# The normalizer of linear attention on VectorE and ScalarE in place of TensorE matmuls and a DRAM broadcast

## The chip, the cores and the metric

The kernel runs on one core of a Trainium2 chip. The metric is the device time of one execution in microseconds (us). "PE" is TensorE, "PEld" its weight loads, "DVE" VectorE, "ACT" ScalarE, "POOL" GpSimd and "SP" SyncE, which only starts DMAs here. Each engine works through its own queue in order; a semaphore holds an instruction until what it reads has been written.

## The reference

```python
x = A_x                                        # 2048 tokens, 512 features
g = sigmoid((x * gate_w).sum(-1, keepdims=True))
# branch a: linear attention, 32 heads of 16
q, k, v = heads(x @ wqkv)
phi = lambda t: where(t > 0, t + 1, exp(t)) + 1e-6
kv  = einsum("bhsd,bhse->bhde", phi(k), v)
z   = einsum("bhsd->bhd", phi(k))
num = einsum("bhqd,bhde->bhqe", phi(q), kv)
den = einsum("bhqd,bhd->bhq", phi(q), z)[..., None] + 1e-6
a   = merge(num / den) @ wo
# branch b: layer norm of x, then an MLP over the tokens (1792 hidden), gelu
b   = transpose(gelu(einsum("bsd,sf->bdf", layernorm(x), w1) + b1) @ w2 + b2)
out = g * a + (1 - g) * b
```

The change concerns `den`: for each token and head, one sum over the head's 16 features of phi(q) times z. The kernel divides phi(q) by it before the last product, which gives the same as dividing num.

## The kernel before, in words

Everything is kept in SBUF. `NT` = 16 tiles of 128 tokens, `ND` = 4 blocks of 128 features (8 heads each), `NF` = 14 blocks of 128 hidden units, `SC` = 512 tokens, `NSC` = 4 chunks of that size. The order on each engine is the order in which the code is written out (`manual_schedule`); nothing reorders it.

1. *K stage* (up to 33.7 us). For each token tile: x @ wk on PE (`k_part`), phi on ACT and DVE (`phi`, L216 to L220) into `pk`, statistics for the layer norm, and, four tiles behind, G = x^T phi(k) (`g_tile`), kept in four PSUM banks and copied to `gT`.
2. *Q loop* (33.7 to 57.9 us). For t = 0..15: three matmuls for the first three hidden blocks (`NB0` = 3, j = 0..2) and one block of q with its phi, into `pqT`, which holds phi(q) with features on partitions and tokens along the free axis: `pqT[:, j, tokens]`. From t = 6 on, `z_add` (L281) adds one tile of phi(k) per step into `zacc`. Behind the loop come the last five `z_add`s (L425) and `z_column` (L426, its body L354 to L369): a transpose in blocks of 32x32, sums and small copies, which give `zcol` (z by feature, on partitions) and `Z32` (z spread so that one column belongs to one head).
3. *Hidden loop* (57.9 to 97.85 us). For j = 3..13: 16 matmuls into a bank `uacc`, then the gelu on ACT (L329) into `uT`. Behind j = 6 stand `kv_matmuls` (64 small matmuls, then the product `kvT` on DVE, L348), `den_matmuls` (16 matmuls of 32 output rows in four column tiles, then a reciprocal on DVE, L404), `w2_matmuls` (16 matmuls of 32x32 tiles, whose weights are `kvT`), the 16 gate sums on DVE (L431), and `rden_chunk` for chunks 0 and 1. `w2_copies` (ACT, L391) follow behind j = 6..9 and give `W2sb`.
4. *Output loop* (97.85 us to the end). For each token tile t: four matmuls of `pqT` with `W2sb` into a bank `aps`, scaled on ACT into `a_sc` (L492); 14 matmuls of `uT` with w2 into a bank `yps`; DVE joins both into `ot` (L505), and a DMA writes it out. `rden_chunk` for chunks 2 and 3 stands behind tiles 1 and 2.

`rden_chunk(c)` brings the reciprocal onto phi(q): the reciprocals, one row per head, go to DRAM once (L440), and for each feature block a DMA on POOL's queue reads 8 rows back with each one repeated over 16 partitions (`rex`, L444); DVE multiplies `pqT` by it (L446).

All PSUM tiles come from one pool of eight banks (`bank`); a matmul that opens a new tile waits until the reader of that bank's earlier tile is through. All matmuls are issued by the helper `mm` and so carry L113; the tile's name tells them apart.

Of the kernel before, what the change touches and what calls it, by code (L numbers as in the profile page):

```python
# [7 lines left out]
ACT = mybir.ActivationFunctionType  # L8
ALU = mybir.AluOpType
AX = mybir.AxisListType  # L10
BF16 = mybir.dt.bfloat16
FP32 = mybir.dt.float32
# [3 lines left out]
def kernel(  # L16
# [13 lines left out]
    nc = tc.nc  # L30
    P = nc.NUM_PARTITIONS
    EPS = 1e-5
    PHI_EPS = 1e-6
    HEAD = 16
# [3 lines left out]
    S, D = X.shape  # L38
    F = B_w1.shape[1]
    NT = S // P  # L40
    ND = D // P
    NF = F // P
    SC = 512
    NSC = S // SC
# [16 lines left out]
    wpool = ctx.enter_context(tc.tile_pool(name="wstream", bufs=4))  # L61
    work = ctx.enter_context(tc.tile_pool(name="work", bufs=3))
    opool = ctx.enter_context(tc.tile_pool(name="opool", bufs=4))
    dpool = ctx.enter_context(tc.tile_pool(name="dpool", bufs=1, space=bass.MemoryType.DRAM))
    ps = ctx.enter_context(tc.tile_pool(name="ps", bufs=8, space=bass.MemoryType.PSUM))

    def keep(shape, dtype, name):
        return persist.tile(shape, dtype, name=name, tag=name)

    def bank(name, dtype=FP32):  # L70
        return ps.tile([P, SC], dtype, name=name, tag="bank")

    xs = keep([P, NT, D], BF16, "xs")
# [6 lines left out]
    pqT = keep([P, ND, S], BF16, "pqT")  # L80
# [1 line left out]
    uT = keep([P, NF, D], BF16, "uT")  # L82
    kvT = keep([P, ND, Q32], BF16, "kvT")
    W2sb = keep([P, ND, D], BF16, "W2sb")
    Z32 = keep([P, ND * 40], BF16, "Z32")
    zacc = keep([P, D], FP32, "zacc")
    zT = keep([P, D], FP32, "zT")
    zpart = keep([P, NZ], FP32, "zpart")
    zquad = keep([Q32, NQ, NZ], FP32, "zquad")
    zsum = keep([Q32, NZ], FP32, "zsum")  # L90
    zcol = keep([P, ND], FP32, "zcol")
    rden = keep([P, SC], BF16, "rden")
    ident = keep([P, P], BF16, "ident")
    maskH = keep([P, 8], BF16, "maskH")
    maskQ = keep([P, 2], BF16, "maskQ")
    gw_b = keep([P, D], BF16, "gw_b")
# [6 lines left out]
    gpre = keep([P, NT], FP32, "gpre")  # L103
# [8 lines left out]
    def mm(o, lhsT, rhs, start, stop, **kw):  # L112
        nc.tensor.matmul(o, lhsT=lhsT, rhs=rhs, start=start, stop=stop, **kw)  # L113
# [29 lines left out]
    for k, q in ((1, nc.scalar), (2, nc.sync), (3, nc.scalar)):  # L143
        load_wk(q, k)
    nc.vector.memset(ones_f[:], 1.0)
    nc.vector.memset(mhalf[:], -0.5)
    nc.vector.memset(Z32[:], 0.0)
    nc.gpsimd.memset(ident[:], 0.0)
    nc.gpsimd.affine_select(
        out=ident[:], in_=ident[:], compare_op=ALU.not_equal, fill=1.0, base=0,  # L150
# [5 lines left out]
        out=maskQ[:], in_=maskH[:].rearrange("p (a m) -> p m a", m=2), op=ALU.max, axis=AX.X  # L156
# [4 lines left out]
        out=xT[:, :, 3 * P : 3 * P + 2],  # L161
        in_=xs[:, 0, 0 : 2 * ND].rearrange("p (k c) -> p k c", k=ND),
# [10 lines left out]
    for c, (j0, nb) in enumerate(w1_chunks):  # L173
        w = wpool.tile([P, NT, FB * P], BF16, name="w1c", tag="wc")
        w1c.append(w)
        for t0 in range(0, NT, 8) if c == 0 else (0,):
            t1 = t0 + 8 if c == 0 else NT
            nc.sync.dma_start(
                out=w[:, t0:t1, : nb * P], in_=w1_view[:, t0:t1, j0 * P : (j0 + nb) * P]
# [148 lines left out]
    def gelu(j, acc):  # L328
        nc.scalar.activation(  # L329
            out=uT[:, j, :], in_=acc[:], func=ACT.Gelu_apprx_tanh, bias=bcol[:, j : j + 1]  # L330
        )
# [22 lines left out]
    def z_column():  # L354
        nc.vector.transpose(out=zT[:], in_=zacc[:])
        nc.vector.tensor_reduce(
            out=zpart[:], in_=zT[:].rearrange("p (b k) -> p b k", k=Q32), op=ALU.add, axis=AX.X
        )
        for q in range(NQ):
            nc.vector.tensor_copy(out=zquad[:, q, :], in_=zpart[q * Q32 : (q + 1) * Q32, :])  # L360
        nc.vector.tensor_reduce(
            out=zsum[:], in_=zquad[:].rearrange("p q b -> p b q"), op=ALU.add, axis=AX.X
        )
        for q in range(NQ):
            nc.vector.tensor_copy(
                out=zcol[q * Q32 : (q + 1) * Q32, :],
                in_=zsum[:].rearrange("p (j q) -> p q j", q=NQ)[:, q, :],
            )
        nc.vector.tensor_tensor(  # L369
            out=Z32[:].rearrange("p (j m) -> p j m", m=40)[:, :, 0:8],  # L370
            in0=zcol[:].unsqueeze(2).to_broadcast([P, ND, 8]),
            in1=maskH[:].unsqueeze(1).to_broadcast([P, ND, 8]), op=ALU.mult,
        )

    w2ps = []

    def w2_matmuls():
        w2ps.extend(bank("w2ps") for _ in range(ND))
        for j in range(ND):
            for i in range(NQ):  # L380
                r, c = i * Q32, (i ^ j) * Q32
                mm(
                    w2ps[j][c : c + Q32, :], kvT[r : r + Q32, j, :], wo_sb[r : r + Q32, j, :],
                    True, True, tile_position=(r, c),
                )

    def w2_copies(j):
        n = Q32 * (NQ, 1, 2, 1)[j]
        for r in range(0, P, n):
            c = (r // Q32 ^ j) * Q32  # L390
            nc.scalar.activation(  # L391
                out=W2sb[r : r + n, j, :], in_=w2ps[j][c : c + n, :], func=ACT.Copy
            )

    def den_matmuls():
        denps = bank("denps")
        for j in range(ND):
            for c in range(NSC):
                mm(
                    denps[32 * c : 32 * c + 32, :], Z32[:, 32 * j : 32 * j + 32], pqT[:, j, c * SC : (c + 1) * SC],  # L400
                    j == 0, j == ND - 1, tile_position=(0, 32 * c),
                )
        with nc.allow_low_precision(reason="the normalizer is used in bf16"):
            nc.vector.reciprocal(out=rden[:], in_=denps[:])  # L404

    NB0 = 3
    accs = [bank("uacc") for _ in range(NB0)]
# [16 lines left out]
    for t in range(11, NT):  # L424
        z_add(t)  # L425
    z_column()  # L426

    def gate_sums():
        for t in range(NT):
            junk = work.tile([P, D], BF16, name="junk", tag="junk", bufs=2)  # L430
            nc.vector.tensor_tensor_reduce(  # L431
                out=junk[:], in0=xs[:, t, :], in1=gw_b[:], scale=1.0, scalar=0.0,
                op0=ALU.mult, op1=ALU.add, accum_out=gpre[:, t : t + 1],
            )

    rd_dram = dpool.tile([P, SC], BF16, name="rd_dram", tag="rd_dram")

    def rden_chunk(c):
        if c == 0:
            nc.gpsimd.dma_start(out=rd_dram[:], in_=rden[:])  # L440
        for j in range(ND):
            rex = work.tile([P, SC], BF16, name="rex", tag="rex", bufs=4)
            src = rd_dram[32 * c + 8 * j : 32 * c + 8 * j + 8, :]
            nc.gpsimd.dma_start(out=rex[:], in_=src.unsqueeze(1).to_broadcast([8, HEAD, SC]))  # L444
            seg = pqT[:, j, c * SC : (c + 1) * SC]
            nc.vector.tensor_tensor(out=seg, in0=seg, in1=rex[:], op=ALU.mult)  # L446

    w2c = []

# [9 lines left out]
    for j in range(NB0, NF):  # L459
        c, jj = divmod(j, FB)  # L460
        acc = bank("uacc")
        for t in range(NT):
            mm(acc[:], w1c[c][:, t, jj * P : (jj + 1) * P], hs[:, t, :], t == 0, t == NT - 1)
        gelu(j, acc)
        if j == NB0 + 3:
            kv_matmuls()
            den_matmuls()
            w2_matmuls()
            gate_sums()
            rden_chunk(0)  # L470
            rden_chunk(1)
        if NB0 + 3 <= j < NB0 + 3 + ND:
            w2_copies(j - NB0 - 3)
        if jj == FB - 1 or j == NF - 1:
            load_w2(c)

# [2 lines left out]
        out=gg[:], in0=gth[:], scalar1=0.5, scalar2=0.5, op0=ALU.mult, op1=ALU.add  # L479
    )  # L480
    nc.vector.tensor_scalar(
        out=c1[:], in0=gth[:], scalar1=-0.5, scalar2=0.5, op0=ALU.mult, op1=ALU.add
# [3 lines left out]
    for t in range(NT):  # L486
        c, tl = divmod(t, TPC)
        aps = bank("aps")
        for j in range(ND):
            mm(aps[:], pqT[:, j, t * P : (t + 1) * P], W2sb[:, j, :], j == 0, j == ND - 1)  # L490
        a_sc = work.tile([P, D], FP32, name="a_sc", tag="a_sc", bufs=2)
        nc.scalar.activation(  # L492
            out=a_sc[:], in_=aps[:], func=ACT.Identity,
            scale=gg[:, t : t + 1], bias=c2[:, t : t + 1],
        )
        for c0, W in ((0, D - P), (D - P, P)) if t == NT - 1 else ((0, D),):
            cs = slice(c0, c0 + W)
            yps = bank("yps")
            for f in range(NF):
                mm(  # L500
                    yps[:, :W], w2c[c][:, f, tl * P : (tl + 1) * P], uT[:, f, cs],
                    f == 0, f == NF - 1,
                )
            ot = opool.tile([P, D], BF16, name="ot", tag="ot")
            nc.vector.scalar_tensor_tensor(  # L505
                out=ot[:, :W], in0=yps[:, :W], scalar=c1[:, t : t + 1], in1=a_sc[:, cs],
                op0=ALU.mult, op1=ALU.add,
            )
            (nc.scalar if t < 2 else nc.sync).dma_start(out=o_view[:, t, cs], in_=ot[:, :W])
        if 0 < t < NSC - 1:  # L510
            rden_chunk(t + 1)


# [28 lines left out]
```

## Time and profile before

| | |
|---|---|
| median of 8 runs | 164.22 us (164.0 to 164.57) |
| the profiled execution's own time | 164.57 us |
| span in its profile, first to last instruction | 162.8 us |
| PE busy | 159.2 us, 98% |
| DVE busy | 89.9 us, 55% |
| ACT busy | 62.8 us, 39% |
| POOL busy | 17.5 us, 11% |
| mean granted TensorE clock | 1.000 |

The busy share is a mean over the span; part 2 of the page cuts the span into 40 slices of 4.07 us and gives each engine's busy share in tenths. The chain that ended last is found backwards from the last instruction: at each step to what released it, or to the instruction before it on its engine. A stall of an engine on that chain, or work added there, moves the end; work beside it does so only if something on the chain comes to wait for it.

### The profile page before, as it was taken

To read this page: it belongs to the slowest core of one execution; us is meant where nothing else is said; L and a number is where in the kernel's file an instruction comes from. 1 tells how busy PE (TensorE), PEld (TensorE's weight loads), DVE (VectorE), ACT (ScalarE), POOL (GpSimd) and SP (SyncE) were. 2 spreads that over 40 slices of the span, in tenths; PEclk is the share of its full clock that TensorE was granted. 3 is DMA by queue.
4 is the path that set the end of the run, shared out by engine and by line. 5 is a ranking of instruction groups with operands and counts; after the bars stand their busy time and mean duration, and the time that the engine had idled before them with its cause. 6 is when DMAs were issued, how large, how long until landed. Compare 5 with 4: busy or idle time off the path is not lost.

```text
span 162.8 us, 2189 instructions
## 1 busy us (share of the span) xinstructions
PE 159.2 (98%) x833; PEld 72.6 (45%) x833; DVE 89.9 (55%) x211; ACT 62.8 (39%) x96; POOL 17.5 (11%) x34
## 2 busy tenths in 40 slices
PE   7999999999999999999999999999999999999993
PEld 2444444444444444444444444444444444444452
DVE  1789999957999999509995401255211111111112
ACT  3264286748667473211865113111122222111110
POOL 3000701200010000001425500050000000000000
PEclk9999999999999999999999999999999999999999
DMA  4999999999900006700892699932000001111001
GB/s 155 219 225 247 284 340 332 378 386 387 333 12 0 0 0 201 249 4 0 257 334 69 198 326 298 327 113 87 32 32 32 32 32 36 46 47 35 32 32 32
DMA packets 30569, 25.18 MB, mean 155 GB/s; under 512 B 8480, under 2 KB 29984, under 8 KB 30560
## 3 DMA queue, kind: packets, MB, share of 16 engines
q1 hardware_dynamic: 28256, 21.89, 43.1%
q0 software_dynamic: 1440, 2.38, 5.5%
q10 hardware_dynamic: 864, 0.79, 1.5%
q8 instruction: 6, 0.10, 0.3%
q14 instruction: 3, 0.02, 0.0%
HBM read 21.11 MB, written 2.23 MB: 143 GB/s over the span
## 4 chain that ended last, share of the span: by engine, by line
PE 98%; DVE 0%; issue 0%
PE uacc L113 30%; PE yps L113 30%; PE kacc L113 9%; PE aps L113 8%; PE qacc L113 8%; PE gacc L113 8%; PE wps L113 2%; PE pt L113 1%; PE denps L113 1%; PE kvps L113 0%; PE w2ps L113 0%; DVE ot L505 0%; PE pt L335 0%
## 5 line engine op out<-in xcount | busy, mean ns | idle before, releaser
L113 PE MATMUL uacc<-hs,w1c 128*128 128x512 bf16 x224 | 51.3, 379 | 0.0
L113 PE MATMUL yps<-uT,w2c 128*128 128x512 bf16 (+2 forms) x238 | 51.0, 366 | 0.0
L505 DVE SCALAR_TENSOR_TENSOR ot<-yps,c,a_sc 128x512 bf16<-128x512 f32 (+2 forms) x17 | 12.2, 719 | 44.4 <-PE yps L113 41.3
L113 PEld LDWEIGHTS <-w2c 128*128 128x128 bf16 x238 | 22.8, 98 | 25.9
L113 PEld LDWEIGHTS <-w1c 128*128 128x128 bf16 x224 | 21.8, 98 | 26.3 <-issue 0.2
L492 ACT ACTIVATE a_sc<-aps,c,gg 128x512 f32<-128x512 f32 x16 | 12.4, 778 | 46.7 <-PE aps L113 39.9
L329 ACT ACTIVATE uT<-uacc,bcol 128x512 bf16<-128x512 f32 x14 | 9.3, 688 | 21.7 <-PE uacc L113 21.7
L113 PE MATMUL kacc<-wk_sb,xT 128*128 128x512 bf16 x64 | 16.7, 396 | 0.0
L113 PE MATMUL aps<-W2sb,pqT 128*128 128x512 bf16 x64 | 16.4, 379 | 0.0
L113 PE MATMUL qacc<-xT,wq_sb 128*128 128x512 bf16 x64 | 16.4, 379 | 0.0
L113 PE MATMUL gacc<-pk,xs 128*128 128x512 bf16 x64 | 15.8, 379 | 0.0
L256 ACT ACTIVATE hs<-xs,nmr,rstd 128x512 bf16<-128x512 bf16 x16 | 12.8, 805 | 1.8 <-DVE nmr L250 1.8
L216 ACT ACTIVATE e<-qacc 128x512 bf16<-128x512 f32 x16 | 9.6, 597 | 9.2 <-PE qacc L113 9.2
L216 ACT ACTIVATE e<-kacc 128x512 bf16<-128x512 f32 x16 | 9.3, 594 | 9.6 <-PE kacc L113 9.5
L444 POOL DMA_DIRECT2D rex<-rd_dram x16 | 9.5, 602 | 22.5 <-DVE pqT L446 20.2
L220 DVE SCALAR_TENSOR_TENSOR pk<-kacc,e 128x512 bf16<-128x512 f32 x16 | 11.1, 692 | 0.6
L220 DVE SCALAR_TENSOR_TENSOR pqT<-qacc,e 128x512 bf16<-128x512 f32 x16 | 11.1, 692 | 0.6
L113 PEld LDWEIGHTS <-xs 128*128 128x128 bf16 x76 | 7.4, 104 | 8.5 <-DMA xs<-in_A_x_dram 0.9
L240 DVE BATCH_NORM_STATS2 stats<-xs 128x6 f32<-128x512 bf16 x16 | 10.9, 682 | 0.0
L217 DVE TENSOR_SCALAR e<-e 128x512 bf16<-128x512 bf16 x32 | 9.0, 282 | 3.3 <-ACT e L216 3.3
L113 PEld LDWEIGHTS <-xT 128*128 128x128 bf16 x64 | 6.3, 100 | 8.3 <-issue 0.7
L431 DVE CUSTOM_DVE_ANT_0 junk<-xs,gw_b 128x512 bf16<-128x512 bf16 x16 | 9.8, 684 | 0.0
(61 smaller groups left out, 73.2 us busy)
## 6 DMA issues: line engine op xcount, KB each, us to landing
w2c<-in_B_w_dram SPq DMA_DIRECT2D x8, 896.0 KB, 6.2
w1c<-in_B_w_dram SPq DMA_DIRECT2D x2, 2048.0 KB, 14.1
w1c<-in_B_w_dram SPq DMA_DIRECT2D x3, 1024.0 KB, 11.2
rex<-rd_dram POOLq DMA_DIRECT2D x16, 128.0 KB, 4.5
out_dram<-ot SPq DMA_DIRECT2D x13, 128.0 KB, 1.7
xs<-in_A_x_dram SPq DMA_DIRECT2D x3, 512.0 KB, 4.3
wq_sb<-in_A_wqkv_dram SPq DMA_DIRECT2D x1, 512.0 KB, 6.1
wv_sb<-in_A_wqkv_dram SPq DMA_DIRECT2D x1, 512.0 KB, 11.4
```

What stands on the lines that cost most here:

```text
L113: nc.tensor.matmul(o, lhsT=lhsT, rhs=rhs, start=start, stop=stop, **kw)
L216: nc.scalar.activation(out=e[:], in_=acc[:], func=ACT.Exp)
L217: nc.vector.tensor_scalar(out=e[:], in0=e[:], scalar1=1.0, scalar2=PHI_EPS, op0=ALU.min, op1=ALU.add)
L220: nc.vector.scalar_tensor_tensor(out=dst, in0=acc[:], scalar=0.0, in1=e[:], op0=ALU.max, op1=ALU.add)
L240: nc.vector.bn_stats(out=stats[:], in_=xs[:, t, :])
L256: nc.scalar.activation(out=hs[:, t, :], in_=xs[:, t, :], func=ACT.Identity, scale=rstd[:, t : t + 1], bias=nmr[:, t : t + 1],)
L329: nc.scalar.activation(out=uT[:, j, :], in_=acc[:], func=ACT.Gelu_apprx_tanh, bias=bcol[:, j : j + 1])
L431: nc.vector.tensor_tensor_reduce(out=junk[:], in0=xs[:, t, :], in1=gw_b[:], scale=1.0, scalar=0.0, op0=ALU.mult, op1=ALU.add, accum_out=gp ...
L444: nc.gpsimd.dma_start(out=rex[:], in_=src.unsqueeze(1).to_broadcast([8, HEAD, SC]))
L492: nc.scalar.activation(out=a_sc[:], in_=aps[:], func=ACT.Identity, scale=gg[:, t : t + 1], bias=c2[:, t : t + 1],)
L505: nc.vector.scalar_tensor_tensor(out=ot[:, :W], in0=yps[:, :W], scalar=c1[:, t : t + 1], in1=a_sc[:, cs], op0=ALU.mult, op1=ALU.add,)
```

## The change

The normalizer is no longer computed by matmuls. For each of the 16 pieces of phi(q) (chunk c of 512 tokens, feature block j) the new function `den_block`

1. multiplies the piece by z per partition on ACT, into an fp32 tile `pz`,
2. transposes `pz` in 32x32 blocks on DVE, so that features lie along the free axis,
3. sums groups of 16 (the heads) and takes the reciprocal of the 32 sums per partition,
4. transposes back, reading each reciprocal 16 times, which spreads it over its head's 16 features, and
5. multiplies `pqT` by it.

`den_matmuls`, `Z32` with its memset and its product in `z_column`, the DRAM tile and `rden_chunk` are gone. In the hidden loop (i = j - 3) `kv_matmuls` stands behind j = 3 and `w2_matmuls` behind j = 4, both formerly behind j = 6; `w2_copies` and the first eight `den_block`s follow from j = 4 on; the gate sums, formerly all behind j = 6, are spread: four behind j = 3, one behind each of the next eight, two behind each of the last two. The other eight `den_block`s stand behind tiles 0 to 7 of the output loop. `z_add` and `z_column` stay where they were.

```diff
-    def den_matmuls():
-        denps = bank("denps")
-        for j in range(ND):
-            for c in range(NSC):
-                mm(
-                    denps[32 * c : 32 * c + 32, :], Z32[:, 32 * j : 32 * j + 32], pqT[:, j, c * SC : (c + 1) * SC],
-                    j == 0, j == ND - 1, tile_position=(0, 32 * c),
-                )
+    def den_block(c, j):
+        seg = pqT[:, j, c * SC : (c + 1) * SC]
+        pz = work.tile([P, SC], FP32, name="pz", tag="pz", bufs=2)
+        nc.scalar.activation(out=pz[:], in_=seg, func=ACT.Copy, scale=zcol[:, j : j + 1])
+        nc.vector.transpose(out=zT[:], in_=pz[:])
+        den = work.tile([P, SC // HEAD], FP32, name="den", tag="den", bufs=1)
+        nc.vector.tensor_reduce(
+            out=den[:], in_=zT[:].rearrange("p (a d) -> p a d", d=HEAD), op=ALU.add, axis=AX.X
+        )
+        rd = work.tile([P, SC // HEAD], BF16, name="rd", tag="rd", bufs=1)
         with nc.allow_low_precision(reason="the normalizer is used in bf16"):
-            nc.vector.reciprocal(out=rden[:], in_=denps[:])
+            nc.vector.reciprocal(out=rd[:], in_=den[:])
+        rex = work.tile([P, SC], BF16, name="rex", tag="rex", bufs=1)
+        nc.vector.transpose(
+            out=rex[:].rearrange("p (a d) -> p a d", d=HEAD),
+            in_=rd[:].unsqueeze(2).to_broadcast([P, SC // HEAD, HEAD]),
+        )
+        nc.vector.tensor_tensor(out=seg, in0=seg, in1=rex[:], op=ALU.mult)
...
@@ in the hidden loop, behind gelu(j, acc)
-        if j == NB0 + 3:
+        i = j - NB0
+        if i == 0:
             kv_matmuls()
-            den_matmuls()
+        elif i == 1:
             w2_matmuls()
-            gate_sums()
-            rden_chunk(0)
-            rden_chunk(1)
-        if NB0 + 3 <= j < NB0 + 3 + ND:
-            w2_copies(j - NB0 - 3)
+        if 1 <= i < 1 + ND:
+            w2_copies(i - 1)
+        if 1 <= i < 1 + 2 * ND:
+            den_block(*divmod(i - 1, ND))
+        for t in range(4 * i, 4 * i + 4) if i < 1 else range(i + 3, i + 4) if i < 9 else range(2 * i - 6, 2 * i - 4):
+            if t < NT:
+                gate_sum(t)
         if jj == FB - 1 or j == NF - 1:
             load_w2(c)
...
@@ at the end of an output tile
-        if 0 < t < NSC - 1:
-            rden_chunk(t + 1)
+        if t < 2 * ND:
+            den_block(*divmod(t + 2 * ND, ND))
```

More of the change, by code (lines that the diff above doesn't have):

```diff
@@ L63 @@
     opool = ctx.enter_context(tc.tile_pool(name="opool", bufs=4))
-    dpool = ctx.enter_context(tc.tile_pool(name="dpool", bufs=1, space=bass.MemoryType.DRAM))
     ps = ctx.enter_context(tc.tile_pool(name="ps", bufs=8, space=bass.MemoryType.PSUM))
@@ L84 @@
     W2sb = keep([P, ND, D], BF16, "W2sb")
-    Z32 = keep([P, ND * 40], BF16, "Z32")
     zacc = keep([P, D], FP32, "zacc")
@@ L91 @@
     zcol = keep([P, ND], FP32, "zcol")
-    rden = keep([P, SC], BF16, "rden")
     ident = keep([P, P], BF16, "ident")
@@ L146 @@
     nc.vector.memset(mhalf[:], -0.5)
-    nc.vector.memset(Z32[:], 0.0)
     nc.gpsimd.memset(ident[:], 0.0)
@@ L368, in z_column @@
             )
[L369 to L372, printed above, removed]
-        )
     w2ps = []
@@ L393, in w2_copies @@
             )
-    def den_matmuls():
-        denps = bank("denps")
-        for j in range(ND):
-            for c in range(NSC):
-                mm(
-                    denps[32 * c : 32 * c + 32, :], Z32[:, 32 * j : 32 * j + 32], pqT[:, j, c * SC : (c + 1) * SC],
-                    j == 0, j == ND - 1, tile_position=(0, 32 * c),
-                )
-        with nc.allow_low_precision(reason="the normalizer is used in bf16"):
-            nc.vector.reciprocal(out=rden[:], in_=denps[:])
+    def den_block(c, j):
[8 more added lines that the diff above has]
+        rd = work.tile([P, SC // HEAD], BF16, name="rd", tag="rd", bufs=1)
+        with nc.allow_low_precision(reason="the normalizer is used in bf16"):
+            nc.vector.reciprocal(out=rd[:], in_=den[:])
[5 more added lines that the diff above has]
+        nc.vector.tensor_tensor(out=seg, in0=seg, in1=rex[:], op=ALU.mult)
     NB0 = 3
@@ L426, with gate_sum @@
     z_column()
[L428 to L446, printed above, removed]
+    def gate_sum(t):
+        junk = work.tile([P, D], BF16, name="junk", tag="junk", bufs=2)
+        nc.vector.tensor_tensor_reduce(
+            out=junk[:], in0=xs[:, t, :], in1=gw_b[:], scale=1.0, scalar=0.0,
+            op0=ALU.mult, op1=ALU.add, accum_out=gpre[:, t : t + 1],
+        )
     w2c = []
```

## The prediction

> **What bounds the kernel now.** I read the page's first two parts, then the chain that ended last in order of time, because only the chain says what a removed matmul is worth.
>
> ```profile
> PE 159.2 (98%) x833; PEld 72.6 (45%) x833; DVE 89.9 (55%) x211; ACT 62.8 (39%) x96; POOL 17.5 (11%) x34
> ...
> DVE  1789999957999999509995401255211111111112
> ```
>
> PE is busy for 98% of the span, VectorE for 55%. But the share is a mean: in the second row VectorE is full until slice 16 (about 65 us) and nearly idle after slice 28. VectorE has room late, and none early. The chain around the change:
>
> ```profile
> 57.92 13.81 PE uacc L113 x64
> 71.73 0.59 PE kvps L113 x64
> 72.32 0.88 PE denps L113 x16
> 73.20 0.36 PE w2ps L113 x16
> 73.57 24.28 PE uacc L113 x112
> 97.85 0.86 PE aps L113 x4
> ```
>
> The columns are start, length, what. PE runs without a gap from the hidden blocks j=3..6 (four of 16 matmuls, 13.81/4 = 3.45 us each) through kvps, denps and w2ps to j=7..13. So PE time taken away here shortens the run by as much, and PE time spent waiting lengthens it by as much. What VectorE does in that stretch, from the timeline:
>
> ```profile
> 60.01 4.31 DVE L281 TENSOR_TENSOR zacc<-zacc,pk 128x512 f32<-128x512 f32 x6
> ...
> 64.36 0.71 DVE L355 STREAM_TRANSPOSE zT<-zacc 128x512 f32<-128x512 f32 x1
> ...
> 65.10 0.69 DVE L356 TENSOR_REDUCE zpart<-zT 128x16 f32<-128x512 f32 x1
> ...
> 66.84 0.68 DVE L365 COPY zcol<-zsum 32x4 f32<-32x4 f32 x4
> 67.55 0.19 DVE L369 TENSOR_TENSOR Z<-zcol,maskH 128x32 bf16<-128x32 f32 x1
> ...
> 72.41 0.29 DVE L348 TENSOR_TENSOR kvT<-kvps,maskQ 128x128 bf16<-128x128 f32 x1 [4.67 <-PE kvps L113]
> ```
>
> VectorE is still adding up z when the q loop is over (57.9), and its z column is done only at 67.74. Then it idles 4.67 us until kvps ends. PE comes to kvps at 71.73, after this backlog: today nobody waits for it. This margin is what the change spends.
>
> [...] the trace has 688 for the gelu (bias pointer) and 805 for hs [...]. [...] the start shows the slow clock (6 warm-up matmuls in 2.72 us, 453 ns each, against 216 later).
>
> **The change, part by part.**
>
> *Removed from PE.* denps, 16 matmuls in four column tiles: 0.88 us of the chain. This is the whole gain on the bounding engine.
>
> *Removed elsewhere.* The 3.36 us reciprocal, the round trip through DRAM (17 DMAs on POOL's queue), Z32 and its memset. None is on the chain; nothing on PE waited for them. Worth nothing.
>
> *Moved.* kv_matmuls goes from behind j=6 to behind j=3, w2_matmuls from behind j=6 to behind j=4. The kvT product (L348), which stands between them, is in VectorE's queue behind all of z_add and z_column, since these are written ahead of the loop; the built order of the changed kernel has it there too: five z_adds, transpose, sums, copies, then kvT, then the gate sums. In the built program the first weight load of w2ps waits for exactly this kvT product.
> PE: 57.92 + 3.45 (j=3) + 0.59 (kvps) + 3.45 (j=4) = 65.41, and there it wants kvT.
> VectorE: nothing ahead of kvT changes except the Z32 product, so zcol ends at 66.84 + 0.68 = 67.52; kvT starts at 67.55 (where the Z32 product stood) and takes 0.29: 67.84. The hop to PE is 0.05 us, from the transposes at the start:
>
> ```profile
> 4.23 0.69 DVE L212 CAST xT<-pt 128x512 bf16<-128x512 f32 x1 [0.49 <-PE pt L113]
> ...
> 4.97 0.10 PEld L113 LDWEIGHTS <-xT 128*128 128x128 bf16 x1 [0.20 <-DVE xT L212]
> ```
>
> So w2ps loads at 67.89, starts at about 67.90, and PE stands for 67.90 - 65.41 = 2.5 us. Everything behind it on PE's queue, j=5..13 and the whole output stage, stands with it. Before, w2ps started at 73.14 by its record, and 162.80 - 73.14 = 89.66 us followed. Now two more blocks (j=5, 6) follow as well: 2 x 3.45 = 6.90. New span 67.90 + 89.66 + 6.90 = 164.46, that is +1.66. That is the stall (+2.5) less denps (-0.88). Anything small that PE loses or gains ahead of w2ps, such as the change of tile shape between kvps and j=4, is swallowed by the stall, whose end VectorE sets.
> wv_sb and wo_sb, wanted 10 and 8 us earlier, were issued at 19.2 and 23.1 and landed 11.4 and 8.8 us later, by 32: no wait. gT is done by 34.6.
>
> *Added on ACT.* 16 pz products. Bounds: 0.60 (the exp, no pointer) to 0.81 (hs); I take 0.71. With gelu 0.69 and the four copies of W2sb at 0.59, blocks i=2 and i=4 hold 0.69 + 2.39 + 0.71 = 3.8 us against PE's 3.45, the next ones 2.6 or 1.4. ACT falls 0.35 behind and recovers. It costs nothing (nor can it gain, as ACT is off the chain): the PSUM bank of a block is asked for again several blocks later. The second table load stays the last one in the built order. pz waits for a buffer that the transpose two blocks earlier frees; behind it stands the next gelu, with over 3 us to spare.
>
> *Added on VectorE.* den_block, 16 times: fp32 transpose 0.71; reduce over 512 elements 0.69 (as zpart); reciprocal of 32 elements, between 0.16 (the zcol copies' row) and 0.35 ((3.36 - 0.15)/512 = 6.3 ns each, plus 0.15), taken 0.35; transpose of a bf16 broadcast, not in the trace: [...] 1.4 if the stride-0 read halves its rate, taken 0.71 [...]; product 0.42. Sum 2.9, and five starts at 0.03: 3.05 us. With a gate sum (0.61) that is 3.7 us a block against PE's 3.45, so VectorE drifts later. It starts den_block at 67.84 + 4 x 0.61 = 70.3, once waits for pz behind the four W2sb copies (to about 75.6), and ends block i=8 near 101, the last gate sum near 104. Then a_sc of tile 0 comes at about 105, when yps of tile 0 has ended at 103.3: the first output tile is 2 us late, but its PSUM banks are asked for only at tile 4 (115). In the output stage VectorE does 0.75 + 3.05 = 3.8 us per tile against 3.88, and the last den_block ends near 138; PE wants it for tile 12, at 97.85 + 1.66 + 12 x 3.885 = 146.1. Cover 8 us, or 0.5 per block: from 3.55 us a block on it costs. Tile 8 (130.6) needs the block that ends near 123. The tail, tile 15, comes after all of it: unchanged.
>
> **Sum.** Profiled execution: 164.57 with a span of 162.8, so 1.77 lies around it; 164.46 + 1.77 = 166.2. That execution is the slowest of the eight, 0.35 over their median; the forecast of the median is 164.22 + 1.66 = 165.9.
>
> **Rivals.**
> *A, no stall: faster.* If kvT is ready when PE has ended j=4, only denps counts: 164.22 - 0.88 = 163.3. It decides at kvT = 66.3, where the stall equals the saving; kvT would have to be 1.5 us earlier than the timeline has it. For it: PE is the chain, and VectorE idles 4.67 us there today. Against: that idling comes after 67.7, and the queue is in order.
> *B, the clock falls in the gap.* [...] Price from the start of this trace: warm-up 2.72 instead of 6 x 0.216 = 1.30, so about +1.4, up to +2.4 with the 20 kacc matmuls behind (5.34 instead of 4.32). About 165.9 + 1.7 = 167.6. For it: the gap; against: [...] PE is dense on both sides.
> *C, VectorE becomes the bound.* With 1.4 for the broadcast transpose, den_block is 3.75: (3.75 - 3.55) x 16 = 3.2 us late for tile 12, about 169. Nothing speaks for a half rate but the unknown.
>
> **How the numbers follow.** Forecast 0.78, its own range 165.4 to 166.4 (the runs shown spread 0.57[...]). B 0.09, C 0.06, A 0.07. The range reaches over B to 167.7; A and C's far end, 0.13, stay out. Faster by over 0.2% (0.33 us, about what a measurement can tell from no change): 0.06 of A. Within: 0.03 (the rest of A and the forecast's low edge). Slower: 0.91.
>
> **What would show it.** Right: a PE gap of about 2.5 us before w2ps near 65.4 in the chain or the waits, released by kvT (L344 there); kvT at 67.6; no denps; j=5 starting near 68.3; aps after it at full pace. Wrong, A: no wait for kvT. B: uacc matmuls of j=5 spaced over 400 ns. C: a wait of PE for pqT ahead of tile 8 or 12, and a transpose row over 1 us. If the gap is there and the time still falls, my sum has missed something in the stretch from 68 to 98.

## The result, and the profile after

The changed kernel takes 165.98 us at the median of 11 executions (165.73 to 167.98), the kernel before 164.09 us (32 executions): a ratio of 1.0136, 95% interval 1.0114 to 1.0157. The change made the kernel slower by 1.9 us, where 165.9 us had been forecast.

The 11 executions fall into two groups, and without them the figures below can't be read. Eight have a mean granted TensorE clock of 1.00 and lie at 165.73 to 166.14, median 165.87; three have 0.99 and lie at 167.28, 167.84 and 167.98. The second group has a cause in this kernel, and the experiments come to it. The profiled execution (165.80 us, span 164.0) is of the first group.

First the page, engines and the row of VectorE over 40 slices:

```profile
PE 157.9 (96%) x817; PEld 72.2 (44%) x817; DVE 124.7 (76%) x272; ACT 72.8 (44%) x112; POOL 7.3 (4%) x17
...
DVE  1799999858999999985999999478999994111112
```

PE has 1.3 us less to do and the run is longer all the same: its share fell from 98% to 96%. VectorE went from 55% to 76%; slices 22 to 33, formerly at 0 to 5 tenths, now stand at 4 to 9. Where PE lost time stands in the list of waits. It has one line for a matmul behind VectorE:

```profile
PE w2ps L110 <- DVE kvT L344: 2.4, 1, 2.4
```

The columns are the time in all, how often, and the longest. One wait of 2.4 us, the one that the prediction names. The chain that ended last shows its inside (start, length, what):

```profile
63.15 0.70 DVE zacc L277
...
63.88 0.72 DVE zT L351
...
64.62 0.70 DVE zpart L352
...
67.06 0.30 DVE kvT L344
67.36 0.04 issue
67.41 0.44 PE w2ps L110 x16
67.84 31.18 PE uacc L110 x144
99.03 0.86 PE aps L110 x4
```

Before, this chain was PE from end to end. Now (followed backwards) it leaves PE at w2ps and goes through kvT, the z column and the z_adds into the q loop: VectorE holds 18% of it. Behind w2ps PE runs without a gap again: 144 matmuls in 31.18 us, 216.5 ns each.

### The profile page after: what moved, and what is told of

It reads as the page before. It is cut to its first block, busy times and chain, and to the rows that moved or that the text cites. A ratio compares the mean times of both kernels' runs of the same rounds, so it can differ in the third digit from the quotient of the medians.

```text
span 164.0 us, 2202 instructions
## 1 busy us (share of the span) xinstructions
PE 157.9 (96%) x817; PEld 72.2 (44%) x817; DVE 124.7 (76%) x272; ACT 72.8 (44%) x112; POOL 7.3 (4%) x17
## 4 chain that ended last, share of the span: by engine, by line
PE 79%; DVE 18%; issue 1%; ACT 0%
PE yps L110 30%; PE uacc L110 20%; PE aps L110 8%; PE gacc L110 8%; PE kacc L110 8%; DVE pqT L216 6%; DVE zacc L277 6%; DVE e L213 2%; PE wps L110 2%; PE qacc L110 2%; DVE stats L236 1%; PE pt L110 1%; DVE zT L351 0%; DVE xT L208 0%; DVE zpart L352 0%
## 5 line engine op out<-in xcount | busy, mean ns | idle before, releaser
L110 PE MATMUL kacc<-wk_sb,xT 128*128 128x512 bf16 x64 | 16.1, 381 | 0.1
L390 DVE STREAM_TRANSPOSE zT<-pz 128x512 f32<-128x512 f32 x16 | 11.3, 705 | 4.3 <-ACT pz L389 4.3
L389 ACT ACTIVATE pz<-pqT,zcol 128x512 f32<-128x512 bf16 x16 | 11.4, 715 | 4.8 <-DVE ot L494 4.7
L399 DVE STREAM_TRANSPOSE rex<-rd 128x512 bf16<-128x512 bf16 x16 | 11.4, 711 | 0.6
L392 DVE TENSOR_REDUCE den<-zT 128x32 f32<-128x512 f32 x16 | 11.0, 686 | 0.6
```

Of the source, the lines that this page charges most:

```text
L389: nc.scalar.activation(out=pz[:], in_=seg, func=ACT.Copy, scale=zcol[:, j : j + 1])
L390: nc.vector.transpose(out=zT[:], in_=pz[:])
L392: nc.vector.tensor_reduce(out=den[:], in_=zT[:].rearrange("p (a d) -> p a d", d=HEAD), op=ALU.add, axis=AX.X)
L399: nc.vector.transpose(out=rex[:].rearrange("p (a d) -> p a d", d=HEAD), in_=rd[:].unsqueeze(2).to_broadcast([P, SC // HEAD, HEAD]),)
```

## The experiments

Three theories stood against each other. S: the time is the wait of w2ps for kvT less the removed denps. L: the added work on VectorE and ACT costs it somewhere else. C: the executions up to 168 us are those in which TensorE's clock fell in the gap. Times are medians; "before" was measured beside each set, 164.0 us for the first four, on one chip, and 164.1 us for the other three, on another.

### w2 one block later

```diff
-        elif i == 1:
+        elif i == 2:
             w2_matmuls()
-        if 1 <= i < 1 + ND:
-            w2_copies(i - 1)
+        if 2 <= i < 2 + ND:
+            w2_copies(i - 2)
```

> The changed kernel with w2_matmuls and its copies one hidden block later (behind j=5 and from j=5 on); everything else, all den_block work included, stays. PE then reaches w2ps near 68.9 by the working of the prediction, after kvT (67.8). Theory S (the time is the wait for kvT less denps): no wait, so before less 0.88 = 163.2 us, ratio 0.995; w2ps in the trace without idle before it. Theory L (the added VectorE and ScalarE work costs the time somewhere else): it stays near 166.0. Theory C (the scatter of the changed kernel up to 168 is TensorE's clock falling in the gap): no execution over 1% above the median here, clock 1.00 in all.

Measured: 163.58 us, ratio 0.997 (0.996 to 0.998), ten executions between 163.22 and 163.90, the lowest clock 0.998. No matmul waits in the hidden loop. All 16 den_blocks are in this kernel, on the same engines, and it is faster than before: theory L is refuted. The time is 0.4 us above the figure of S; 0.1 of that stands where PE changes from uacc to w2ps (61.40 to 68.41 in the timeline, 7.01 us for 32 matmuls of 216 ns, 6.91), the rest stays open.

### kvT first

```diff
-    for t in range(11, NT):
-        z_add(t)
-    z_column()
...
         if i == 0:
             kv_matmuls()
+            for t in range(11, NT):
+                z_add(t)
+            z_column()
```

> The changed kernel with the last five z_adds and z_column behind the kvT product in VectorE's queue (kv_matmuls is written first, then they follow, still behind j=3). PE's order is that of the changed kernel: w2ps behind j=4. kvT then waits only for kvps and ends near 62.3; zcol comes about 1.3 us later (near 68.9), and with it the den_blocks. Theory S: no wait at w2ps, 163.2 us, ratio 0.995, as with w2 later. Theory L: near 166.0 or above, as VectorE's work is the same and later. Theory C: no scatter to 168.

Measured: 163.39 us, ratio 0.9959 (0.9945 to 0.9973), clocks 0.998 and above. The timeline, VectorE and then PE:

```profile
61.55 0.29 DVE L344 TENSOR_TENSOR kvT<-kvps,maskQ 128x128 bf16<-128x128 f32 x1 [1.36 <-PE kvps L110]
61.76 3.58 DVE L277 TENSOR_TENSOR zacc<-zacc,pk 128x512 f32<-128x512 f32 x5
```

```profile
61.40 3.63 PE L110 MATMUL uacc<-hs,w1c 128*128 128x512 bf16 x15
64.95 0.43 PE L110 MATMUL w2ps<-wo_sb,kvT 32*32 32x512 bf16 x16
```

kvT is done at 61.84, PE comes to w2ps at 64.95 and finds it ready. A change of order alone, with the same work on every engine, is worth 2.5 us against the full-clock executions of the changed kernel (165.87), which is the wait. This is the fastest version measured, and faster than before by 0.6 us.

### The moves alone

The kernel before, with `kv_matmuls` and `w2_matmuls` moved as in the change, and nothing else:

```diff
-        if j == NB0 + 3:
+        if j == NB0:
             kv_matmuls()
-            den_matmuls()
+        if j == NB0 + 1:
             w2_matmuls()
+        if j == NB0 + 3:
+            den_matmuls()
...
-        if NB0 + 3 <= j < NB0 + 3 + ND:
-            w2_copies(j - NB0 - 3)
+        if NB0 + 1 <= j < NB0 + 1 + ND:
+            w2_copies(j - NB0 - 1)
```

> The kernel before with the moves alone: kv_matmuls behind j=3, w2_matmuls behind j=4 and its copies from there; den_matmuls, the gate sums and the broadcast through DRAM stay behind j=6. Theory S: kvT now stands behind z_column and the Z32 product and ends near 68.0, PE waits about 2.7 us, and denps is still there: 164.1 + 2.7 = 166.8 us, slower than the changed kernel by 0.9. Theory L: no den_block here, so about 164.1. Theory C: executions with a clock of 0.99 and 1.5 to 2 us more appear here too, as in the changed kernel, in roughly a quarter.

Measured: three executions with clock 1.00 at 166.80, 166.88 and 167.05, three with 0.99 at 168.14, 168.26 and 168.70; all six together give a ratio of 1.0217 (1.0181 to 1.0253). The full-clock group is 2.9 us over before, where 2.7 were expected. The wait in the trace:

```profile
67.69 0.66 PE L113 MATMUL w2ps<-wo_sb,kvT 32*32 32x512 bf16 x16 [2.47 <-DVE kvT L348]
```

So the moves, without a single den_block, make the loss, and more than it: denps, which this kernel keeps (0.98 us in its chain), is about what lies between it and the changed kernel (166.88 and 165.87). The profiled execution had the lower clock. Its stretches (length, then busy time of PE, PEld, DVE, ACT and POOL, the granted clock, the DMA share and GB/s):

```profile
64.00:68.00 4.00, 1.53 (x22) 0.52 (x20) 3.35 (x14) 0.69 (x1) 0.00 (x0) 0.96 0.97 324
68.00:72.00 4.00, 4.00 (x27) 1.43 (x12) 0.00 (x0) 0.60 (x1) 0.00 (x0) 0.62 0.02 7
72.00:76.00 4.00, 3.95 (x19) 1.85 (x19) 0.00 (x0) 2.63 (x5) 0.00 (x0) 1.00 0.00 0
```

and the same middle stretch of the changed kernel's profiled execution:

```profile
68.00:72.00 4.00, 4.00 (x20) 1.86 (x19) 3.90 (x10) 1.62 (x3) 0.00 (x0) 1.00 0.02 5
```

PE is busy in both for all 4 us, but here with a granted clock of 0.62: right behind the gap the clock is down. By an estimate from the clocks of the first two stretches, 4 us x (0.38 + 0.04) = 1.7 us of PE are lost; in the chain, w2ps and the 19 uacc behind it take 0.66 + 5.57 = 6.23 us, where 0.44 and 19 x 0.2165 of the changed kernel make 4.55. That is about what separates the two groups (1.3 to 1.8 us). The matmuls of this stretch, by tile:

```profile
L113 PE MATMUL uacc<-hs,w1c x11: 379/606/634, 68.3 to 71.8; 128*128 128x512 bf16 x11
```

Their median is 606 ns (the middle of three); in the changed kernel, at a clock of 1.00, it is 379 in the same stretch.

### A longer gap

```diff
         z_add(t)
+    for _ in range(2):
+        nc.vector.tensor_tensor(out=zT[:], in0=zacc[:], in1=pk[:, 0, :], op=ALU.add)
     z_column()
```

> The changed kernel with two more fp32 sums of 0.685 us on VectorE ahead of z_column, into a scratch tile that z_column overwrites; they add nothing to the result. kvT and w2ps come 1.4 us later, the gap on PE is 3.8 us instead of 2.4. Theory S: 165.9 + 1.4 = 167.3 us in executions with the full clock. Theory C: the longer gap lets the clock fall in most or all executions, so the median is 168.5 to 169.5 and the clock 0.99; if the clock has nothing to do with the gap, the median is 167.3 and the share of slow-clock executions stays a quarter. Theory L: about 166.0, as VectorE has room later.

Measured: 168.92 us, ratio 1.0325 (1.0292 to 1.0358). All six executions have a lowered clock: four with 0.99 at 168.82 to 168.93, two with 0.98 at 170.31 and 170.11. The page's clock row, in tenths over 40 slices, has the dip where the gap ends:

```profile
PEclk9999999999999999779999999999999999999999
```

The wait itself grew as S has it, to 3.8 us for 2.4:

```profile
PE w2ps L110 <- DVE kvT L344: 3.8, 1, 3.8
```

What lies over 167.3 us, 1.6 us in four executions and 2.9 in two, goes with the lower clock. No trace of an execution with 0.98 was kept.

### A shorter gap

w2 behind 6 of the 16 matmuls of j = 5 (its copies behind j = 5 to 8):

```diff
         for t in range(NT):
+            if j == NB0 + 2 and t == 6:
+                w2_matmuls()
             mm(acc[:], w1c[c][:, t, jj * P : (jj + 1) * P], hs[:, t, :], t == 0, t == NT - 1)
...
-        elif i == 1:
-            w2_matmuls()
-        if 1 <= i < 1 + ND:
-            w2_copies(i - 1)
+        if 2 <= i < 2 + ND:
+            w2_copies(i - 2)
```

> The changed kernel with w2_matmuls 6 of the 16 matmuls into hidden block j=5, so that PE comes to them 1.3 us later: a gap of 1.1 us in place of 2.4; its copies stand behind j=5 to j=8. Theory S: one gap of about 1.1 us released by kvT; the time lies 1.3 under the full-clock executions of the changed kernel, 165.9 - 1.3 = 164.6 us, about 0.6 over before. Theory C (the clock falls only if the gap fills enough of some fixed stretch of time, which 2.4 us does now and then and 3.8 us always does): no execution here with a clock under 0.995. If any gap at all could lower the clock, some would have 0.99.

```profile
67.48 0.44 PE L110 MATMUL w2ps<-wo_sb,kvT 32*32 32x512 bf16 x16 [1.07 <-DVE kvT L344]
```

Measured: 164.74 us, ratio 1.0037 (1.0025 to 1.0048); the wait is 1.07 us, and none of the eleven executions is below a clock of 0.998. With the others, two of them told further down, this makes a row by the length of the gap:

```
gap of PE    executions with a clock of 0.99 or less
none         0 of 38   (w2 later, kvT first, den matmuls back)
1.1 us       0 of 11   (this one)
1.3, 1.7 us  0 of 5    (two gaps, the heavier den_block)
2.4 us       3 of 11   (the changed kernel)
2.5 us       3 of 6    (the moves alone)
3.8 us       6 of 6
```

So the executions of the changed kernel up to 168 us, all with a clock of 0.99, go with the gap, and come and go with its length. Two limits of this row: the gaps of 2.5 and 3.8 us were measured on one chip and those of 1.1 to 1.7 us on the other (no gap: 16 executions on the first, 22 on the second; the changed kernel's chip is not on record), so no chip is known to show both sides of the limit. And a long time is not always the clock: one execution without a gap (166.84 us, the den matmuls back) and one of before (165.96 us) had a clock of 1.00; why they were long stays open.

The kept traces point to why 2.4 us may be a matter of chance. The two drops on trace last 3.41 us each, at half the clock. The full clock stands as one entry in the clock's record, 157.01 us long before and 160.43 us in the changed kernel: 46.0 and 47.0 times 3.413 us. Here are two stretches of that length around w2ps, the second being the drop; for the changed kernel they are counted off from the start of its entry (5.26 us, so that the 18th ends at 66.70). The first number behind the length is PE's busy time, the third from the end the clock. The moves alone:

```profile
64.24:67.66 3.42, 0.98 (x5) 0.25 (x3) 3.15 (x13) 0.69 (x1) 0.00 (x0) 1.00 1.03 346
67.66:71.07 3.41, 3.38 (x23) 1.18 (x24) 0.00 (x0) 0.60 (x1) 0.00 (x0) 0.50 0.04 15
```

the longer gap:

```profile
65.87:69.29 3.42, 0.58 (x17) 0.26 (x18) 3.17 (x15) 0.14 (x1) 0.00 (x0) 1.00 0.45 151
69.29:72.70 3.41, 3.41 (x9) 1.22 (x8) 3.34 (x9) 1.07 (x2) 0.00 (x0) 0.50 0.00 0
```

and the changed kernel, whose profiled execution kept its clock:

```profile
63.28:66.70 3.42, 1.76 (x9) 0.59 (x6) 3.18 (x11) 0.69 (x1) 0.00 (x0) 1.00 1.08 367
66.70:70.11 3.41, 2.71 (x27) 1.23 (x28) 3.37 (x12) 1.21 (x2) 0.00 (x0) 1.00 0.26 85
```

PE was idle for 2.4 and 2.8 us of the stretch ahead of a drop. In the changed kernel its 2.4 us fall on two stretches, 1.7 and 0.7, and no drop follows; the gaps of the shorter gap and the heavier den_block are no longer than 1.07 and 1.65 us each. So in these traces a drop came behind 2.4 and 2.8 us of idle time inside one stretch, and none behind 1.7 us or less. That this also sorts the executions of which no trace was kept is not shown.

### A heavier den_block

On top of kvT first, the fp32 transpose of each den_block done twice:

```diff
         nc.vector.transpose(out=zT[:], in_=pz[:])
+        nc.vector.transpose(out=zT[:], in_=pz[:])
```

> The arrangement with kvT first (163.4 us), with the fp32 transpose of each den_block done twice; the result is the same. A den_block then takes 2.94 + 0.74 = 3.68 us on VectorE. The prediction put the cover at 3.55 us a block. In the trace with kvT first, the last den_block ends at 134.9 and PE wants it at about 143.8, so 8.9 us of cover against 16 x 0.74 = 11.8 us of added work: theory V (VectorE's cover is a sum over all blocks up to tile 12) expects PE to wait about 2 to 3 us for pqT ahead of tiles 8 to 12, 165.4 to 166.5 us. Against it: if VectorE's blocks are covered singly (3.68 + 0.75 over a tile's 3.88), the lateness would show from the first output tiles on and the time would be over 168; if they had no limit near, 163.4.

Measured: 166.96 us, ratio 1.0175 (1.0156 to 1.0194), 3.6 us over kvT first. PE now waits twice, each time for the last pqT piece of a chunk, at tile 8 and at tile 12:

```profile
129.72 0.39 PE L110 MATMUL aps<-W2sb,pqT 128*128 128x512 bf16 x1 [1.31 <-DVE pqT L404]
...
147.09 0.39 PE L110 MATMUL aps<-W2sb,pqT 128*128 128x512 bf16 x1 [1.65 <-DVE pqT L404]
```

The idle times sum to 2.96 us. By the starts of the matmuls the loss is somewhat larger: three `aps` start at 127.60 and three at 144.63, 216 ns apart, so the fourth is 1.47 and 1.81 us late, 3.3 us in all. The median lies 0.5 us over the upper end of the expectation, and this difference is most of it. VectorE's cover is a sum over the blocks, as theory V has it: of the 11.8 us of added work, about 8.5 are swallowed. The tiles in between do not wait, although VectorE is late there too.

### The den matmuls back

On top of kvT first, 16 matmuls of the size of the old denps behind j = 6, read by nobody:

```diff
+        elif i == 3:
+            extra = bank("extra")
+            for jx in range(ND):
+                for cx in range(NSC):
+                    mm(
+                        extra[32 * cx : 32 * cx + 32, :], wv_sb[:, jx, 0:32], xT[:, jx, cx * SC : (cx + 1) * SC],
+                        jx == 0, jx == ND - 1, tile_position=(0, 32 * cx),
+                    )
```

> The arrangement with kvT first (163.4 us), with 16 matmuls of the size and tiling of the old denps put back on PE behind j=6; they read wv_sb and xT and nobody reads what they write, so the result is the same. If the removed matmuls were worth their 0.88 us, plus 0.1 for two more changes of tile shape: 164.3 to 164.4 us, a little above the kernel before. If they were hidden beside other work: 163.4.

Measured: 164.71 us, ratio to before 1.0027 (1.0014 to 1.0041), so 1.1 us more than kvT first by the two ratios. Their place in the chain:

```profile
72.80 0.98 PE extra L110 x16
73.78 24.28 PE uacc L110 x112
```

The matmuls stand on the chain with 0.98 us, and 112 matmuls behind them take 24.28 in place of 31.18 x 112/144 = 24.25. From the start of j = 3 to the first `aps` the chain takes 40.24 us (57.82 to 98.06), with kvT first 39.15 (57.42 to 96.57): 1.09 more, which is what the ratios give. So putting such matmuls back costs 0.2 us beyond their 0.88, where 0.1 was expected: they take 0.98, and the 32 uacc ahead of them 7.01 in place of 6.91 (216 ns each); the rest of the 0.3 us by which the median lies over the expectation is within the intervals. Removing denps was worth about what the prediction took.

## Why the prediction was right, point by point

*The stall.* 2.5 us were forecast, 2.37 measured. The missing 0.1 stands at the change of tile shape: with kvT first, where nothing waits, the 16 matmuls between kvps and w2ps take 3.56 us (61.46 to 65.02 in the chain) in place of 3.45, so PE comes to w2ps that much later. As the prediction says, this is swallowed by the wait, since VectorE sets its end. kvT ended at 67.35 instead of 67.84, because this execution reached the q loop's end 0.5 us earlier (57.42 for 57.92): in the profiled execution of before, the matmuls at the start were slow for longer (the first 20 kacc took 5.40 us, here 4.91; mean of all kacc 396 ns, here 381). That is also why the span came out at 164.0 and not 164.46. From the record of j = 3 to that of the first aps the traces have 39.93 us before (57.76 to 97.69) and 41.60 after (57.27 to 98.87): +1.67, forecast +1.66. The medians moved by 1.9 us, 1.8 with the full-clock group alone; this 0.1 to 0.2 more stays open. That the median hit 165.9 to 0.1 us is in part luck, since the kernel before came out 0.13 us below the 164.22 that the forecast started from.

*What follows the stall.* Nine blocks of 3.45 us and the output loop at full pace: from w2ps (67.41) to the first aps (98.87 by its record) 31.46 us, forecast 31.45.

*The gain.* denps was put at 0.88 us. Taken out without the stall it gives less. With kvT first the chain from j = 3 to the first aps is 39.15 us against 39.93 before, 0.78 less: the 0.88, and 0.1 back for one more change of tile shape (the 3.56 us in place of 3.45), since there is no stall to swallow it. Rival A's forecast of 163.3 missed that term. From the 164.0 of that set it gives 163.2, and 163.4 was measured; the last 0.2 stays open.

*Rival A* needed kvT by 66.3 (65.8 in the profile after, which reached the loop 0.5 us earlier), and it came at 67.35 behind five z_adds and the z column. The second experiment is what A describes, with the order turned round.

*Rival B, the clock.* It was put at 0.09 and struck in 3 of 11 executions, too few to set the median. The dip itself is on trace in the moves alone and in the longer gap; of the changed kernel's three only the mean clock was kept. Its price was right (1.4 to 2.1 us over the full-clock median; 1.7 forecast), for a reason that the working did not have: the drops on trace are 3.41 us at half the clock, by an estimate from these two numbers a loss of 1.7. That the forecast held against it is in part luck too. With a gap of nearly the same length the moves alone lost the clock in 3 of 6, and there the median lies between the groups. That a gap of 2.5 us is too short for a drop was an assumption of the prediction; no trace had shown it. The measurement decides: with 2.4 us, 3 of 11 executions have the lower clock; with up to 1.7 us, none of 16.

*VectorE's load, rival C.* den_block was put at 3.05 us with one unknown, the transpose of a broadcast. The page of the changed kernel settles it (busy time, mean ns of one, idle before):

```profile
L390 DVE STREAM_TRANSPOSE zT<-pz 128x512 f32<-128x512 f32 x16 | 11.3, 705 | 4.3 <-ACT pz L389 4.3
L389 ACT ACTIVATE pz<-pqT,zcol 128x512 f32<-128x512 bf16 x16 | 11.4, 715 | 4.8 <-DVE ot L494 4.7
L399 DVE STREAM_TRANSPOSE rex<-rd 128x512 bf16<-128x512 bf16 x16 | 11.4, 711 | 0.6
```

The bf16 transpose with its repeated read takes 711 ns, the fp32 one 705. The two differ by under 1%, neither half nor double: the 0.71 us taken for it, which no trace had shown, was an estimate that held. ACT's product takes 715 ns, against the 0.71 us taken between the 0.60 of the exp and the 0.81 of hs. A den_block takes 2.94 us (69.71 to 72.65). VectorE's lateness went nearly as forecast: a wait for pz behind the four W2sb copies to 75.32 (forecast 75.6), the last gate sum at 102.7 (104), the last den_block at 135.7 (138), with PE wanting it at about 146. Two more waits for pz, 1.18 us each at the first two output tiles, were not in the working; the shorter den_block made up for them. The heavier den_block shows that this cover ends, and roughly where.

## What to carry to other kernels

When PE is the chain, an instruction removed from it is worth about its length (here 0.78 us in the chain for the 0.88 of denps) only if the operands of everything that PE then reaches earlier are still early enough: write down, for every matmul that is moved forward, when the other engine's queue delivers its operand. A step that feeds PE belongs in front of a backlog in an in-order queue, not behind it: kvT started at 67.06 us behind the z column and at 61.55 ahead of it, and the same work in that other order was worth 2.5 us. And, as far as these runs go, count a gap of 2.4 us or more on PE twice: once for its length, and once for the clock it may cost (1.3 to 2.1 us, in 6 of 17 executions at 2.4 to 2.5 us).

## What the runs showed of the hardware

With a gap of 2.4 to 2.5 us on PE the granted clock was 0.99 in 6 of 17 executions, with one of 3.8 us 0.98 or 0.99 in 6 of 6; with gaps of 1.1 to 1.7 us it was 0.998 or more in all 16. The two drops on trace last 3.41 us, at half the clock; PE had been idle for 2.4 and 2.8 us of the 3.42 us before. In the changed kernel's trace, with at most 1.7 us idle in one such stretch, the clock stayed at 1.00. The executions with the lower clock took 1.3 to 2.1 us longer, two behind the longest gap 2.9. At a clock of 1.00 the 128x512 matmuls of a hidden block ran at 216.5 ns each (144 behind w2ps in 31.18 us); where they give way to small tiles and PE waits for nothing, 0.1 us more passed (3.56 us in place of 3.45 with kvT first, 7.01 in place of 6.91 ahead of the den matmuls put back), and those den matmuls took 0.98 us, where denps took 0.88 before. A transpose of 128x512 on VectorE took 705 ns in fp32 and 711 in bf16 with each element read 16 times.
